# Softmax attention with an FFN behind it: three moves in the tail of a tile's work, and a new order in two steps of nine

## The chip, the cores and the metric

One core of a Trainium2 chip runs the whole kernel. The metric is the device time of one execution in microseconds (us). TensorE (PE, with its weight loads as PEld), VectorE (DVE), ScalarE (ACT), GpSimd (POOL) and SyncE (SP, which issues the DMAs) each work through their own instructions in the order in which the program gives them, and wait for each other by semaphores.

## The reference

Attention for 4 batches and 8 heads, 576 positions, head size 64, with a relative bias from a small network, and a two-layer FFN (512 to 2048 to 512, leaky ReLU) on its output:

```python
scores = scale * np.matmul(q, k.transpose(0, 1, 3, 2)) + bias     # bias: MLP of log-distances, per head
scores = scores - np.max(scores, axis=-1, keepdims=True)
attn = np.exp(scores)
attn = attn / (np.sum(attn, axis=-1, keepdims=True) + 1e-09)
attn_out = np.matmul(attn, v)
# attn_out -> x [2304, 512]
h = x @ w_in
out = np.maximum(0.01 * h, h) @ w_out
```

## The kernel before, in words

A unit is one pair of heads of one batch; there are 16 units (4 head pairs, 4 batches each, the batch running fastest). The 2 x 576 query rows of a unit are cut into nine tiles of 128 rows: A0 B0 A1 B1 M A2 B2 A3 B3 (A and B are the two heads; M holds the last 64 rows of both). `step(n)` is called for n = 0 to 152 and works on three tiles at once. "Step 0" to "step 8" below are n modulo 9.

In a step, TensorE makes the scores of tile n (`qk_mm`, L235; L227 for M). VectorE adds the bias and finds the extremum in one pass (`softmax_a`, L258). ScalarE takes the exponential and its row sums (`softmax_b`, L266). Three steps later `transposes` turns the tile on TensorE (L300, L304, L318) into a PSUM tile `t`, which ScalarE copies to `PT` (L316, L306).

After the first five tiles (M is the last of them) and after the last four (B3 is the last) a half unit is complete. `recip` makes the reciprocals of the row sums on VectorE (L272 adds 1e-9, L273 inverts), and GpSimd spreads them over a tile `rb` (L276, L278) and copies a piece of M (L279). `turn_rb` turns `rb` on TensorE (L305, L289) into the upper half of the PSUM tile `o`, and VectorE copies it to `PT` (L309 twice for M, L290). Then `pv` multiplies with V (L335, 20 matmuls) into the same PSUM tile `o`, columns 0 to 287. L290 reads the whole of that tile. A PV group is issued in step 0 and in step 4, one each. `pv_exit` scales the result on VectorE (L348) a step later.

The first 512 positions of batch 0 (both exits of units 0, 4, 8 and 12) go into FFN block 0's own tiles at once. For them `pv_exit` scales into `xt` (L344), ScalarE rounds it (L345, `hi`), and a step later VectorE subtracts to get the rest (L386, `lo`).

The order is written out by hand. In most steps scores and softmax come first, then transposes and PV. Step 4 (`ahead`) has transposes and PV first. Beside this, step 1 rounds the next unit's q (L194, VectorE) and steps 2 and 3 subtract its rest (L206, GpSimd); step 4 rounds k (L199) and steps 5 and 6 subtract its rest (L209, GpSimd). Three VectorE or ScalarE pieces of the weights' preparation (`fill`) come at the end of step 0 and in step 4. PSUM tiles `s` (scores), `t` and `o` have two buffers each. Before all this the bias tables are made (the first 65 us or so); behind it the FFN runs, its first matmul group (`ffn1(0, 0)`) being issued after step n = 146.

Of the kernel before, what the change touches and what calls it, by code (L numbers as in the profile page):

```python
# [8 lines left out]
F32 = mybir.dt.float32  # L9
# [5 lines left out]
B, H, S, D, HID = 4, 8, 576, 64, 32  # L15
# [10 lines left out]
KINDS = ["A0", "B0", "A1", "B1", "M", "A2", "B2", "A3", "B3"]  # L26
# [3 lines left out]
LAG = 3  # L30
# [6 lines left out]
def attention_ffn(ctx: ExitStack, tc: tile.TileContext, qt, kt, vm, vt, wi, wo, cst, out):  # L37
    nc = tc.nc
# [12 lines left out]
    def pstile(tag):  # L51
        shape = [128, 1024] if tag == "s" else [128, 512]
        return ps.tile(shape, F32, tag=tag, name="ps_" + tag)
# [3 lines left out]
    ident = ap.tile([128, 128], F32, name="ident")  # L57
# [7 lines left out]
    PT = ap.tile([128, 2, 10, HS], F32, name="PT")  # L65
# [23 lines left out]
    def gen_w(T):  # L89
        return max(S - 16 * T, 16 * T + 16)  # L90

    plan, load = [], {"a": 0.0, "v": 5.0}
    for T in GEN:
        w = gen_w(T)
# [79 lines left out]
    def load_unit(u):  # L174
        hp, b = divmod(u, B)
        q_, k_ = raw_b[u % 2]
        for t, src in ((q_, qt), (k_, kt)):
            for p in (0, 64):
                nc.sync.dma_start(out=t[p:p + 64], in_=src[hp, b])
        raw[u] = (q_, k_)  # L180
# [30 lines left out]
    st, pp = {}, {}  # L211

    def tile_id(n):
        u, i = divmod(n, 9)
        return u, KINDS[i]
# [22 lines left out]
    mx_t, sm_t, rb_t, pair = {}, {}, {}, [None]  # L238

    def softmax_a(n):  # L240
        u, kind = tile_id(n)
        hp = u // B
        bt = bias[hp, "M"][:] if kind == "M" else bias[hp, kind[1]][:, 0 if kind[0] == "A" else 1, :]
        col = 1 if kind[0] == "B" else 0
        if col == 0:
            mx_t[n] = ap.tile([128, 2], F32, tag="mx", name="mx", bufs=6)
        else:
            mx_t[n] = mx_t[n - 1]
        g, sc = int(KINDS.index(kind) > 4), 4 if kind == "M" else 2 * (int(kind[1]) % 2) + col
        if kind in ("A0", "A2"):  # L250
            sm_t[u, g] = ap.tile([128, 12], F32, tag="sm", name="sm", bufs=3)
        if kind == "M":
            pair[0] = ap.tile([128, S + 64], F32, tag="pM", name="pM", bufs=1)
        elif col == 0:
            pair[0] = ap.tile([128, 2 * S], F32, tag="p", name="p", bufs=3)
        p = pair[0][:, S * col:S * col + S]
        s_, i = st.pop(n), mx_t[n][:, col:col + 1]
        nc.vector.tensor_tensor_reduce(out=p, in0=s_[:, S0:S0 + S], in1=bt, scale=-0.125, scalar=3.4e38, op0=ALU.add, op1=ALU.min, accum_out=i)  # L258
        pp[n] = pair[0]
        ex_q.append((p, i, sm_t[u, g][:, sc:sc + 1]))  # L260
# [3 lines left out]
    def softmax_b():  # L264
        p, i, sm = ex_q.pop(0)
        nc.scalar.activation(out=p, in_=p, func=AF.Exp, bias=i, scale=-1.0, accum_out=sm)  # L266

    def recip(n):
        u, kind = tile_id(n)
        g = int(kind != "M")  # L270
        sm, w = sm_t.pop((u, g)), 4 if g else 5
        nc.vector.tensor_scalar_add(sm[:, 0:w], sm[:, 0:w], 1e-9)  # L272
        nc.vector.reciprocal(sm[:, 6:6 + w], sm[:, 0:w])  # L273
        rb = rb_t[u, g] = ap.tile([128, 384], F32, tag="rb", name="rb", bufs=2)
        one = sm[:, 6:10].rearrange("p (h o) -> p h o", o=1).to_broadcast([128, 4, 64])
        nc.gpsimd.tensor_copy(rb[:, 0:256].rearrange("p (h c) -> p h c", h=4), one)  # L276
        if g == 0:
            nc.gpsimd.tensor_copy(rb[:, 256:384], sm[:, 10:11].to_broadcast([128, 128]))  # L278
            nc.gpsimd.tensor_copy(pp[n][:, S:S + 64], pp[n][:, S - 64:S])  # L279

    outs = {}
    pv_q = []

    def halves(t):
        return t[:].rearrange("p (a c) -> p a c", a=2)

    def turn_rb(u, g, rb):
        for i in range(2):
            nc.tensor.transpose(outs[u, g][:, 256 + 128 * i:384 + 128 * i], rb[:, 128 * i:128 * i + 128], ident[:])  # L289
        nc.vector.tensor_copy(PT[:, g, 8:10, 0:256], halves(outs[u, g]))  # L290

    def transposes(n, at):
        u, kind = tile_id(n)
        p = pp.pop(n)
        p0 = S + 64 if kind[0] == "B" else 0
        if kind in ("A0", "M"):
            outs[u, int(kind == "M")] = pstile("o")
        t0 = pstile("t")
        for jb in range(4):
            nc.tensor.transpose(t0[:, 128 * jb:128 * jb + 128], p[:, p0 + 128 * jb:p0 + 128 * jb + 128], ident[:])  # L300
        if kind == "M":
            rb = rb_t.pop((u, 0))
            tl = outs[u, 1]
            nc.tensor.transpose(tl[:, 0:128], p[:, 512:640], ident[:])  # L304
            nc.tensor.transpose(tl[:, 256:384], rb[:, 256:384], ident[:])  # L305
            nc.scalar.copy(out=PT[:, :, 0:8, 256:288], in_=t0[:].rearrange("p (j g c) -> p g j c", j=8, g=2))  # L306
            for h in range(2):
                r, c = slice(64 * h, 64 * h + 64), slice(64 * h, 64 * h + 64)
                nc.vector.tensor_copy(PT[r, :, 8:10, 256:288], halves(tl)[r, :, c].rearrange("p a (g c) -> p g a c", g=2))  # L309
            turn_rb(u, 0, rb)  # L310
            pv_q.append((at, u, 0))
            return
        ic, h = int(kind[1]), 0 if kind[0] == "A" else 1
        g, i2 = ic // 2, ic % 2
        c = slice(128 * i2, 128 * i2 + 128)
        nc.scalar.copy(out=PT[:, g, 0:8, c].rearrange("p (j h) c -> p j h c", h=2)[:, :, h, :], in_=t0[:].rearrange("p (j c) -> p j c", j=4))  # L316
        if h == 1:
            nc.tensor.transpose(outs[u, g][:, c], p[:, 512:640], ident[:])  # L318
            if kind == "B3":
                turn_rb(u, 1, rb_t.pop((u, 1)))  # L320
                pv_q.append((at, u, 1))

    x_pend, pv_out = [], []

    def pv():
        _, u, g = pv_q.pop(0)
        hp, b = divmod(u, B)
        o, pt = outs.pop((u, g)), PT[:, g]
        for jb in range(5):
            for h in range(2):  # L330
                if jb < 4:
                    l, r = vv[u][:, jb, 64 * h:64 * h + 64], pt[:, 2 * jb + h, :]
                else:
                    l, r = vt_b[u % 3][:, h, :], pt[:, 8, :]
                nc.tensor.matmul(o[64 * h:64 * h + 64, 0:HS], l, r, start=(jb == 0), stop=(jb == 4))  # L335
        pv_out.append((hp, S * b + HS * g, o, pt[:, 9, :]))

    def pv_exit():
        hp, t0, o, r = pv_out.pop(0)
        c = max(0, min(HS, BLK - t0))  # L340
        if c:
            x = ap.tile([128, HS], F32, tag="xt", name="xt", bufs=2)
            hi, lo = (t[:, t0:t0 + c] for t in xs[0, hp])
            nc.vector.tensor_mul(x[:, 0:c], o[:, 0:c], r[:, 0:c])  # L344
            nc.scalar.copy(out=hi, in_=x[:, 0:c])  # L345
            x_pend.append((lo, x[:, 0:c], hi))
        if c < HS:
            nc.vector.tensor_mul(x1[hp][:, t0 + c - BLK:t0 + HS - BLK], o[:, c:HS], r[:, c:HS])  # L348

    NTILE = 9 * HP * B  # L350

# [8 lines left out]
    def split(n, when):  # L360
        if n // 9 + 1 < HP * B:
            for f, *args in SPL.get(when, ()):
                (split_hi, split_lo)[f](n // 9 + 1, *args)

    def step(n):
        ahead = n % 9 == 4
        for turn in (ahead, not ahead):
            if turn:
                if 0 <= n - LAG < NTILE:
                    transposes(n - LAG, n + 2)  # L370
                if pv_q and pv_q[0][0] <= n:
                    pv()
                continue
            if n < NTILE:
                qk_mm(n)
                if ahead and n // 9 + 2 < HP * B:
                    load_unit(n // 9 + 2)
                if ahead:
                    split(n, "M")
                    fill(n, 3)  # L380
                softmax_a(n)
            if 0 <= n - 1 < NTILE and KINDS[(n - 1) % 9] in ("M", "B3"):
                recip(n - 1)
            while x_pend:
                lo, x, hi = x_pend.pop(0)
                nc.vector.tensor_sub(lo, x, hi.bitcast(F32))  # L386
            while pv_out and not ahead:
                pv_exit()
        while ex_q:
            softmax_b()  # L390
# [113 lines left out]
    with tc.manual_schedule():  # L504
# [6 lines left out]
        for n in range(NTILE + LAG + 6):  # L511
            u, i = divmod(n, 9)
            if u == 0:
                while done < GEN_AT[i]:
                    gen_tick(done)
                    done += 1
                    if done >= 6 and done % 2 == 0 and sp_ops:
                        w = sp_ops.pop(0)
# [25 lines left out]
            if u < HP * B:  # L544
                if u % B == B - 1 and u // B + 1 < HP:
                    c = {1: "0", 2: "1", 3: "M", 4: "2", 6: "3"}.get(i)
# [41 lines left out]
        for j in range(len(seq) + 2):  # L588
            if j < len(seq):
                n, m = seq[j]  # L590
# [58 lines left out]
```

## Time and profile before

| | us |
|---|---|
| median of 3 runs (719.26 to 720.31) | 720.21 |
| the profiled execution's own time | 719.8 |
| its span in the trace | 718.0 |
| PE busy | 698.7 |
| PEld busy | 544.2 |
| DVE busy | 388.8 |
| ACT busy | 362.6 |
| POOL busy | 111.9 |

The span is 1.8 us shorter than the execution. Matmuls are pipelined and their ends are modelled, so "busy" for PE means that work was in flight. The granted clock of TensorE is at full speed in every slice of the span.

### The profile page before, as it was taken

The page shows a single profiled execution, that of the slowest core. Times are in us where ns is not written, and L with a number is a line of the kernel's source. Part 1 is how long each engine was busy: PE and PEld are TensorE (multiplying, and loading weights), DVE is VectorE, ACT ScalarE, POOL GpSimd, SP SyncE. Part 2 cuts the span into 40 slices and gives each one's busy share as a digit, 9 for nine tenths or more (in the row PEclk, how much of TensorE's full clock was granted, in tenths as well). Part 3 has the DMA queues.
Part 4 walks back from the last instruction along what each step waited for, and adds up shares of the span by engine and source line. Part 5 has one row for each costly group of instructions (what it writes and reads, how often), then busy time and mean ns, then how long its engine had stood idle before and what let it go on. Part 6 is the DMA issues. An engine that isn't in the chain of part 4 may idle for free.

```text
span 718.0 us, 11142 instructions
## 1 busy us (share of the span) xinstructions
PE 698.7 (97%) x4192; PEld 544.2 (76%) x4192; DVE 388.8 (54%) x882; ACT 362.6 (50%) x792; POOL 111.9 (16%) x135
## 2 busy tenths in 40 slices
PE   6999999999999999999999999999999999999997
PEld 2346677777767786767888888888888888888996
DVE  7996789898889889749996211122111221112111
ACT  7797778767778777775563221222211231122221
POOL 2103335333444434300000000000000000000000
PEclk9999999999999999999999999999999999999999
DMA  9798557447755864002550010000000010000100
GB/s 231 239 316 243 167 164 226 115 114 214 211 158 127 244 173 125 21 1 65 173 174 29 1 59 0 1 0 30 31 0 1 0 59 1 0 1 1 59 1 30
DMA packets 30262, 68.26 MB, mean 95 GB/s; under 512 B 8192, under 2 KB 8320, under 8 KB 30208
## 3 DMA queue, kind: packets, MB, share of 16 engines
q1 hardware_dynamic: 30208, 67.54, 32.4%
q8 instruction: 33, 0.54, 0.3%
q14 instruction: 21, 0.17, 0.1%
HBM read 51.92 MB, written 15.61 MB: 94 GB/s over the span
## 4 chain that ended last, share of the span: by engine, by line
PE 85%; DVE 9%; ACT 3%; issue 2%; DMA 1%; DVEq 0%; SPq 0%
PE ps_o L466 13%; PE ps_t L466 13%; PE ps_o L335 10%; PE ps_s L494 9%; PE ps_s L493 9%; PE ps_s L492 9%; PE ps_s L235 7%; PE ps_t L300 6%; DVE r L114 2%; PE ps_o L125 2%; PE ps_t L125 1%; DVE p L258 1%; PE ps_s L227 1%; PE ps_s L125 1%; DVE pM L258 1%
## 5 line engine op out<-in xcount | busy, mean ns | idle before, releaser
L481 DVE TENSOR_TENSOR gl<-g,gh 128x512 fp32r<-128x512 f32 (+1 forms) x80 | 51.0, 638 | 266.2 <-ACT g L475 266.2
L494 PE MATMUL ps_s<-woh,gl 128*128 128x512 f32 x288 | 112.1, 389 | 0.3 <-DVE gl L481 0.3
L492 PE MATMUL ps_s<-woh,gh 128*128 128x512 f32 x288 | 112.2, 390 | 0.0
L493 PE MATMUL ps_s<-wol,gh 128*128 128x512 f32 x288 | 112.2, 390 | 0.0
L266 ACT ACTIVATE p<-p,mx 128x576 f32<-128x576 f32 x128 | 100.0, 781 | 7.6 <-DVE mx L258 7.6
L258 DVE CUSTOM_DVE_ANT_0 p<-ps_s,bias 128x576 f32<-128x576 f32 x128 | 94.0, 750 | 15.0 <-PE ps_s L235 12.5
L235 PE MATMUL ps_s<-ks,qs 128*128 128x288 f32 x512 | 99.9, 318 | 1.8 <-DVE mx L258 1.5
L235 PEld LDWEIGHTS ps_s<-ks,qs 128*128 128x128 f32 x512 | 72.1, 189 | 19.5 <-issue 6.0
L474 ACT ACTIVATE gh<-ps_o 128x512 fp32r<-128x512 f32 (+1 forms) x39 | 21.5, 552 | 126.6 <-PE ps_o L466 126.6
L316 ACT COPY PT<-ps_t 128x512 f32<-128x512 f32 x128 | 73.4, 574 | 12.9 <-PE ps_t L300 12.9
L474 ACT ACTIVATE gh<-ps_t 128x512 fp32r<-128x512 f32 (+1 forms) x39 | 21.5, 552 | 112.0 <-PE ps_t L466 111.9
L300 PE MATMUL ps_t<-ident,p 128*128 128x128 f32 x512 | 75.0, 273 | 2.3 <-ACT PT L316 2.3
L335 PE MATMUL ps_o<-PT,v 128*64 128x288 f32 x512 | 69.2, 412 | 0.3
L300 PEld LDWEIGHTS ps_t<-ident,p 128*128 128x128 f32 x512 | 61.1, 140 | 4.5 <-ACT PT L316 3.6
L494 PEld LDWEIGHTS ps_s<-woh,gl 128*128 128x128 f32 x288 | 54.1, 188 | 12.0 <-DVE gl L481 0.7
L492 PEld LDWEIGHTS ps_s<-woh,gh 128*128 128x128 f32 x288 | 54.1, 188 | 10.8
L493 PEld LDWEIGHTS ps_s<-wol,gh 128*128 128x128 f32 x288 | 54.1, 188 | 10.6
L466 PE MATMUL ps_t<-xh,wil 128*128 128x512 f32 (+1 forms) x156 | 57.3, 367 | 0.0
L466 PE MATMUL ps_o<-xh,wil 128*128 128x512 f32 (+1 forms) x156 | 57.3, 367 | 0.0
L466 PE MATMUL ps_t<-xl,wih 128*128 128x512 f32 (+1 forms) x156 | 57.3, 367 | 0.0
L466 PE MATMUL ps_o<-xl,wih 128*128 128x512 f32 (+1 forms) x156 | 57.3, 367 | 0.0
L466 PE MATMUL ps_t<-xh,wih 128*128 128x512 f32 (+1 forms) x156 | 57.2, 367 | 0.0
(109 smaller groups left out, 1098.8 us busy)
## 6 DMA issues: line engine op xcount, KB each, us to landing
raw<-kt SPq DMA_DIRECT2D x32, 304.0 KB, 5.7
raw<-qt SPq DMA_DIRECT2D x32, 288.0 KB, 4.2
raw<-wi SPq DMA_DIRECT2D x16, 512.0 KB, 3.5
raw<-wo SPq DMA_DIRECT2D x16, 512.0 KB, 3.6
scr<-x SPq DMA_DIRECT2D x21, 295.5 KB, 4.2
bias<-scr SPq DMA_DIRECT2D x16, 288.0 KB, 5.4
out<-x SPq DMA_DIRECT2D x18, 256.0 KB, 2.1
v<-vm SPq DMA_DIRECT2D x16, 256.0 KB, 6.3
```

Of the source, the lines that this page charges most:

```text
L235: nc.tensor.matmul(s_[:, S0 + HS * hh:S0 + HS * hh + HS], qs[:, c0:c0 + 128], ks[:, k0 + HS * hh:k0 + HS * hh + HS], start=(j == 0), stop= ...
L258: nc.vector.tensor_tensor_reduce(out=p, in0=s_[:, S0:S0 + S], in1=bt, scale=-0.125, scalar=3.4e38, op0=ALU.add, op1=ALU.min, accum_out=i)
L266: nc.scalar.activation(out=p, in_=p, func=AF.Exp, bias=i, scale=-1.0, accum_out=sm)
L300: nc.tensor.transpose(t0[:, 128 * jb:128 * jb + 128], p[:, p0 + 128 * jb:p0 + 128 * jb + 128], ident[:])
L316: nc.scalar.copy(out=PT[:, g, 0:8, c].rearrange("p (j h) c -> p j h c", h=2)[:, :, h, :], in_=t0[:].rearrange("p (j c) -> p j c", j=4))
L335: nc.tensor.matmul(o[64 * h:64 * h + 64, 0:HS], l, r, start=(jb == 0), stop=(jb == 4))
L466: nc.tensor.matmul(h_[:, :N], w, x[:, :N], start=(j == 0), stop=(j == len(mms) - 1))
L474: nc.scalar.activation(out=gh[:, :N], in_=h_[:, :N], func=AF.Prelu, alpha=0.01)
L481: nc.vector.tensor_sub(gl[:, :N], g[:, :N], gh[:, :N].bitcast(F32))
L492: nc.tensor.matmul(o, gh[:, c], wt[m][2][:], start=(m == 0), stop=False)
L493: nc.tensor.matmul(o, gh[:, c], wt[m][3][:], start=False, stop=False)
L494: nc.tensor.matmul(o, gl[:, c], wt[m][2][:], start=False, stop=(m == MF - 1))
```

## The change

- `recip` is split. The addition of 1e-9 and the copy of M's piece go to a new `sums`, on GpSimd, in the step in which `recip` was; the reciprocals and the spreading of `rb` come one step later (steps 6 and 1 instead of 5 and 0).
- `turn_rb` comes one step later too (steps 8 and 3 instead of 7 and 2), with its VectorE copies (L309, L290). The PV groups stay in steps 0 and 4.
- In steps 1 and 5 (`behind`) transposes, and then `pv_exit`, stand ahead of the scores.
- `x_steps` replaces the old rounding: the ScalarE copy `hi` comes later in its step's order (behind the transposes' copy), the subtraction `lo` a step after it on GpSimd instead of VectorE.

```diff
+    def sums(n):
+        ...
+        nc.gpsimd.tensor_scalar_add(sm[:, 0:w], sm[:, 0:w], 1e-9)
+        if g == 0:
+            nc.gpsimd.tensor_copy(pp[n][:, S:S + 64], pp[n][:, S - 64:S])
     def recip(n):
-        nc.vector.tensor_scalar_add(sm[:, 0:w], sm[:, 0:w], 1e-9)
         nc.vector.reciprocal(sm[:, 6:6 + w], sm[:, 0:w])
         ...
-            nc.gpsimd.tensor_copy(pp[n][:, S:S + 64], pp[n][:, S - 64:S])
-    def turn_rb(u, g, rb):
+    def turn_rb(n, at):
+        ...
+        rb = rb_t.pop((u, g))
+        if g == 0:
+            tl = outs[u, 1]
+            nc.tensor.transpose(tl[:, 256:384], rb[:, 256:384], ident[:])
+            for h in range(2):
+                ...
+                nc.vector.tensor_copy(PT[r, :, 8:10, 256:288], ...)
         for i in range(2):
             nc.tensor.transpose(outs[u, g][:, 256 + 128 * i:384 + 128 * i], ...)
         nc.vector.tensor_copy(PT[:, g, 8:10, 0:256], halves(outs[u, g]))
+        pv_q.append((at, u, g))
@@ pv_exit
-            nc.scalar.copy(out=hi, in_=x[:, 0:c])
+    def x_steps(n):
+        while x_lo:
+            lo, x, hi = x_lo.pop(0)
+            nc.gpsimd.tensor_sub(lo, x, hi.bitcast(F32))
+        while x_pend:
+            lo, x, hi = x_pend.pop(0)
+            nc.scalar.copy(out=hi, in_=x)
+            x_lo.append((lo, x, hi))
@@ step
-        ahead = n % 9 == 4
-        for turn in (ahead, not ahead):
+        ahead, behind = n % 9 == 4, n % 9 in (1, 5)
+        for turn in (ahead or behind, not (ahead or behind)):
             if turn:
                 if 0 <= n - LAG < NTILE:
-                    transposes(n - LAG, n + 2)
+                    transposes(n - LAG)
+                if 0 <= n - LAG - 1 < NTILE and KINDS[(n - LAG - 1) % 9] in ("M", "B3"):
+                    turn_rb(n - LAG - 1, n + 1)
                 if pv_q and pv_q[0][0] <= n:
                     pv()
                 continue
+            while pv_out and behind:
+                pv_exit()
             if n < NTILE:
                 qk_mm(n)
                 ...
                 softmax_a(n)
+            if 0 <= n - 2 < NTILE and KINDS[(n - 2) % 9] in ("M", "B3"):
+                recip(n - 2)
             if 0 <= n - 1 < NTILE and KINDS[(n - 1) % 9] in ("M", "B3"):
-                recip(n - 1)
-            while x_pend:
-                lo, x, hi = x_pend.pop(0)
-                nc.vector.tensor_sub(lo, x, hi.bitcast(F32))
+                sums(n - 1)
+            x_steps(n)
             while pv_out and not ahead:
                 pv_exit()
```

## Rows read from the trace of the kernel before

**Rows 1.** Windows (us; busy by engine; clock, DMA share, GB/s): nine ordinary steps; nine with unit 8's x exits.
```profile
183.03:198.79 15.76, 15.76 (x129) 12.22 (x130) 13.95 (x36) 12.07 (x30) 6.67 (x9) 1.00 0.71 207
198.79:216.59 17.80, 16.50 (x129) 12.23 (x130) 15.40 (x37) 12.62 (x31) 7.20 (x9) 1.00 0.56 156
```
**Rows 2.** Chain that ended last (start, us, what): first and last step-0 PV groups.
```profile
101.98 2.58 PE ps_o L335 x20
...
313.00 2.58 PE ps_o L335 x20
```
**Rows 3.** Timeline (start, us, instruction, idle before), steps 1 to 4.
```profile
185.54 0.56 PEld L235 LDWEIGHTS ps_s<-ks,qs 128*128 128x128 f32 x4 [0.44 <-DVE tmp L434]
...
186.05 0.49 PEld L300 LDWEIGHTS ps_t<-ident,p 128*128 128x128 f32 x4
...
186.38 0.76 DVE L258 CUSTOM_DVE_ANT_0 p<-ps_s,bias 128x576 f32<-128x576 f32 x1 [0.52 <-PE ps_s L235]
186.50 0.57 PEld L235 LDWEIGHTS ps_s<-ks,qs 128*128 128x128 f32 x4
...
187.06 0.45 DVE L348 TENSOR_TENSOR x<-ps_o,PT 128x288 f32<-128x288 f32 x1
...
187.43 0.68 DVE L194 CAST qs<-raw 128x1024 fp32r<-128x1024 f32 x1
...
188.03 0.75 DVE L258 CUSTOM_DVE_ANT_0 p<-ps_s,bias 128x576 f32<-128x576 f32 x1
...
188.70 0.69 DVE L290 COPY PT<-ps_o 128x512 f32<-128x512 f32 x1
...
189.52 1.65 PEld L335 LDWEIGHTS ps_o<-PT,v 128*64 128x64 f32 x16 [0.17 <-DVE PT L290]
```
**Rows 4.** Timeline, steps 4 to 0 of the same unit.
```profile
192.10 0.21 PEld L227 LDWEIGHTS ps_s<-raw,raw 64*64 64x64 f32 x8 [0.44 <-issue]
...
193.81 0.78 ACT L266 ACTIVATE pM<-pM,mx 128x576 f32<-128x576 f32 x1 [1.75 <-DVE mx L258]
...
194.91 0.19 DVE L273 RECIPROCAL sm<-sm 128x5 f32<-128x5 f32 x1
...
195.02 0.42 DVE L348 TENSOR_TENSOR x<-ps_o,PT 128x288 f32<-128x288 f32 x1
...
195.23 0.40 POOL L276 COPY rb<-sm 128x256 f32<-128x256 f32 x1 [4.37 <-DVE sm L273]
...
195.81 0.24 POOL L279 COPY pM<-pM 128x64 f32<-128x64 f32 x1
...
196.00 2.96 POOL L209 TENSOR_TENSOR ks<-raw,ks 128x576 fp32r<-128x576 f32 x2
...
196.10 0.14 PEld L304 LDWEIGHTS ps_o<-ident,pM 128*128 128x128 f32 x1 [0.22 <-POOL pM L279]
...
196.70 0.59 DVE L309 COPY PT<-ps_o 64x128 f32<-64x128 f32 x2
...
198.72 1.65 PEld L335 LDWEIGHTS ps_o<-PT,v 128*64 128x64 f32 x16 [0.17 <-DVE mx L258]
```
**Rows 5.** Timeline, steps 1 to 4 of unit 9, with unit 8's x exit.
```profile
203.31 0.43 ACT L345 CAST xh<-xt 128x288 fp32r<-128x288 f32 x1 [2.43 <-DVE xt L344]
...
204.47 1.23 DVE L386 TENSOR_TENSOR xl<-xt,xh 128x288 fp32r<-128x288 f32 x1
...
205.62 0.68 DVE L290 COPY PT<-ps_o 128x512 f32<-128x512 f32 x1
...
206.35 1.65 PEld L335 LDWEIGHTS ps_o<-PT,v 128*64 128x64 f32 x16 [0.30 <-DVE PT L290]
```
**Rows 6.** Lines of POOL (busy us, mean ns): the one small addition or product.
```profile
L85 POOL TENSOR_SCALAR cs<-cs 128x32 f32<-128x32 f32 x1 | 0.6, 601 | 2.2 <-DMA cs<-cst 2.2
```
**Rows 7.** Timeline, the last PV group behind the FFN's first matmuls.
```profile
316.44 0.25 PEld L289 LDWEIGHTS ps_o<-ident,rb 128*128 128x128 f32 x2
...
319.63 1.65 PEld L335 LDWEIGHTS ps_o<-PT,v 128*64 128x64 f32 x16 [0.35 <-ACT woh L444]
```

More of the change, by code (lines that the diff above doesn't have):

```diff
@@ L266, in softmax_b @@
         nc.scalar.activation(out=p, in_=p, func=AF.Exp, bias=i, scale=-1.0, accum_out=sm)
+    def sums(n):
+        u, kind = tile_id(n)
+        g = int(kind != "M")
+        sm, w = sm_t[u, g], 4 if g else 5
+        nc.gpsimd.tensor_scalar_add(sm[:, 0:w], sm[:, 0:w], 1e-9)
+        if g == 0:
+            nc.gpsimd.tensor_copy(pp[n][:, S:S + 64], pp[n][:, S - 64:S])
     def recip(n):
@@ L285, in halves @@
         return t[:].rearrange("p (a c) -> p a c", a=2)
-    def turn_rb(u, g, rb):
+    def turn_rb(n, at):
+        u, kind = tile_id(n)
+        g = int(kind != "M")
+        rb = rb_t.pop((u, g))
[3 more added lines that the diff above has]
+            for h in range(2):
+                r, c = slice(64 * h, 64 * h + 64), slice(64 * h, 64 * h + 64)
+                nc.vector.tensor_copy(PT[r, :, 8:10, 256:288], halves(tl)[r, :, c].rearrange("p a (g c) -> p g a c", g=2))
         for i in range(2):
@@ L290, in turn_rb, with transposes @@
         nc.vector.tensor_copy(PT[:, g, 8:10, 0:256], halves(outs[u, g]))
-    def transposes(n, at):
+        pv_q.append((at, u, g))
+    def transposes(n):
         u, kind = tile_id(n)
@@ L301, in transposes @@
         if kind == "M":
[L302 to L305, printed above, removed]
+            nc.tensor.transpose(outs[u, 1][:, 0:128], p[:, 512:640], ident[:])
             nc.scalar.copy(out=PT[:, :, 0:8, 256:288], in_=t0[:].rearrange("p (j g c) -> p g j c", j=8, g=2))
[L307 to L311, printed above, removed]
             return
@@ L318, in transposes @@
             nc.tensor.transpose(outs[u, g][:, c], p[:, 512:640], ident[:])
-            if kind == "B3":
-                turn_rb(u, 1, rb_t.pop((u, 1)))
-                pv_q.append((at, u, 1))
     x_pend, pv_out = [], []
@@ L348, in pv_exit @@
             nc.vector.tensor_mul(x1[hp][:, t0 + c - BLK:t0 + HS - BLK], o[:, c:HS], r[:, c:HS])
+    x_lo = []
+    def x_steps(n):
[6 more added lines that the diff above has]
+            x_lo.append((lo, x, hi))
     NTILE = 9 * HP * B
```

## The prediction

> **What bounds the kernel now.** I read the windows first, with their borders at the PV groups of step 0. Nine ordinary steps take 15.76 us, and PE has work in flight for all of it, while DVE is busy for 13.95 [rows 1]. The nine steps that hold the x exits of unit 8 take 17.80 us for the same 129 matmul records, and there PE is in flight for 16.50 only [rows 1]. The chain that ended last shows how many there are of each: from the step-0 group at 101.98 to that at 313.00 it is 211.0 us for 13 intervals [rows 2]; with three x intervals (units 4, 8, 12) at 17.80, the other ten come to 157.6, or 15.76 each. So attention runs at PE's pace, with DVE little behind, and four units (unit 0 too) lose some 2.0 us each to the x work. A stall of PE is not made up anywhere: it adds to the time.
>
> The timeline shows where a stall is near. I count from P, where PE's weight loads are free of the step-0 group (185.54). The next PV group, in step 4, starts at P + 3.98 (189.52). DVE's L290 ends 0.13 us before it, at P + 3.85 (188.70 + 0.69) [rows 3]. That the group waits for L290 is seen beside unit 8's exits: L290 ends at 206.30, the group starts at 206.35, with an idle time of 0.30 put down to L290 [rows 5]. The code has the reason: L290 reads the whole PSUM tile `o` into whose columns 0 to 287 the group's first matmul writes. So **L290 has 0.13 us to spare, and 0.05 is used by the semaphore**.
>
> **First half: from the step-0 group to the step-4 group.** The diff moves L290 behind the softmax pass of step 3 on DVE, puts the reciprocal ahead of the rounding of q in step 1, and lets the scores of step 1 wait for a set of transposes. The old chain on DVE is: softmax 1 starts at P + 0.84, then L348, L194, softmax 2, L290. The new one, with slots read as start to start [rows 3]:
>
> - four transposes first: 186.05 to 186.50, 0.45; the scores are then 0.84 from done: softmax 1 starts at P + 1.29;
> - softmax 1: 186.38 to 187.06, 0.68, to 1.97;
> - the reciprocal, 194.91 to 195.02, 0.11 [rows 4], to 2.08;
> - L194: 187.43 to 188.03, 0.60, to 2.68;
> - softmax 2: 188.03 to 188.70, 0.67, to 3.35;
> - softmax 3, as softmax 1, 0.68, to 4.03 (its scores are ready earlier: PE has done two sets of scores and two of transposes by 2.05, the third set's end is at 2.05 + 0.84 = 2.89);
> - L290, 0.69, to 4.72, and the semaphore, 0.05: the group starts at P + 4.77.
>
> L348 drops out of this chain, since it now runs while PE transposes. PE itself gets to the group no later than at P + 3.98: nothing was added to its work. So PE **stalls for 4.77 - 3.98 = 0.79 us** in each ordinary unit. What the bounds are: if the reciprocal counts with its full 0.19 [rows 4] it is 0.87; if L290 could go in the gap ahead of softmax 3 (it can't by the order) it would be 0.1. I take 0.79.
>
> **Second half: from the step-4 group to the step-0 group.** I count from Q, where PE is free of the step-4 group (192.10); the step-0 group starts at Q + 6.62 (198.72) [rows 4]. Two things go well. The 0.22 us for which L304 waits on GpSimd's copy L279 goes [rows 4], since that copy now stands ahead of `rb`; and DVE no longer waits for ScalarE ahead of L272, which frees DVE, not PE.
>
> What comes late is `rb`. GpSimd's order was L276, L278, L279 and then twice L209 [rows 4]. Now it is the addition and L279 (step 5), the first L209 (end of step 5), L276 and L278 (step 6), the second L209. The exponential of M ends at 193.81 + 0.78 and 0.1 for its sum: Q + 2.58 [rows 4]. The addition of 128x5 on GpSimd is nowhere in the trace. The nearest rows are the copy of 128x64, 0.24 [rows 4], and a product of 128x32, 0.60 [rows 6]; I take 0.24, as with five columns it is nearer to the smaller, and keep 0.1 to 0.6. With 0.05 for the semaphore it ends at 2.87, L279 at 3.11, the first L209 (half of 2.96) at 4.59, L276 and L278 (195.23 to 195.81, and 0.06 to the end) at 5.23. PE would be at the turned reciprocals by about Q + 4.85: 196.10 is Q + 4.00, less the wait of 0.22, with one M transpose (0.11, a quarter of a set), one set of scores (0.51) and one of transposes (0.45) behind it [rows 3, 4]. It stalls there until 5.28. Then 0.11 for a transpose and 0.33 until DVE reads (186.05 to 186.38 [rows 3]), L309 twice, 0.59, L290, 0.69, and 0.05: the group starts at 7.05, late by 0.43. If the addition takes 0.6, it is 0.79; if `rb` is there in time, DVE's own order (softmax 8 until about 5.37, then 0.59, 0.69, 0.05) still gives 6.70, late by 0.08. I take 0.45, with 0.08 to 0.79.
>
> No DMA is issued by a moved step, and SP's queue is as before. Behind the waiting addition stand both L209; the second ends near Q + 6.8, and its k is first used in step 1 of the next unit, after P. In the first half the same moves cost nothing on GpSimd: `rb` of B3 is asked for at P + 3.0, and GpSimd has nothing else from the reciprocal (2.1) on.
>
> An ordinary unit thus costs **0.79 + 0.45 = 1.24 us more**, 17.0 instead of 15.76.
>
> **The x exits.** Before, ScalarE's copy `hi` waits 2.43 us for DVE's L344 at the head of ScalarE's queue, the next transposes' copy stands behind it, and the subtraction L386 holds DVE for 1.23 us ahead of L290 [rows 5]. After, L344 is early, `hi` stands behind the transposes' copy, and the subtraction is on GpSimd. From L209's 128x576 (1.48) 288 columns are 0.74, an estimate; GpSimd is busy for 6.67 of 15.76 [rows 1], so it fits. Then these four intervals become ordinary ones at 17.0: 17.80 - 17.00 = 0.80 less each, **3.2 us less**. The bound on the other side is that 0.7 us of GpSimd work ahead of `rb` makes an x interval 0.7 longer: 2.8 in all.
>
> A rule of the Trainium skill bears on this (SBUF — State Buffer, "SBUF: two separate sides"): one pair of SBUF ports is shared by VectorE and GpSimd, and whichever of an instruction of GpSimd and one of VectorE with two SBUF inputs (or in a two-port mode) starts first holds it, while the other stands still. The trace agrees as far as it goes: L386 has two SBUF inputs and takes 1.23 us beside L206, L348 of the same size reads PSUM and takes 0.45 [rows 3, 5]. What it would do to the reciprocal is the second rival.
>
> **The ends.** The last unit has no next q and k to round: in its first half the chain ends 0.4 to 0.6 earlier, in its second `rb` is in time. Some 0.7 in all, by the same sums. The last group of all stood behind the FFN's first matmuls, with its turned `rb` ahead of them at 316.44 [rows 7]; now its transposes come behind them, 0.22 before 319.63, and 0.3 for their end, 0.69 for L290, 0.05: it starts near 320.6 instead of 319.63, 0.95 later. The FFN behind it is as before and moves as a whole. The work ahead of the first step-0 group is bound by the bias tables; I put it at nothing, within 0.5 both ways.
>
> **The sum.** Ten ordinary intervals (nine of those ten from 101.98 on, and the one ahead of them): 10 x 1.24 = 12.4. Four x intervals: -3.2. Last unit 0.7, last group 0.95. In all +10.9 us on the profiled execution's own 719.8 (span 718.0 and 1.8 around it): 730.7; the median of the runs is 0.4 above that execution. I predict **731.0 us**.
>
> **Rivals.**
>
> 1. *The reciprocal is held by the port too.* The reciprocal of step 6 comes while the first L209 runs (Q + 3.11 to 4.59). If it must wait for its end, then softmax 7 starts at 4.70, softmax 8 ends at 6.06, L309 and L290 at 7.34, and the group starts at 7.39 instead of 7.05. That is 0.34 more for 14 units: 735.8. For it: L386's 1.23 us. Against: no row shows a one-input operation of five columns beside GpSimd.
> 2. *`rb` in time.* GpSimd is quicker, or PE later, than I have it: only 0.08 is lost in the second half. 10 x 0.87 - 4 x 1.17 + 0.6 + 0.95 = +5.6: 725.4. For it: the margin is only 0.4 us.
> 3. *Faster.* The mechanism: L290 keeps up. DVE had 0.52 us idle ahead of softmax 1 [rows 3] and gets rid of L272's waits and of L386; if that let it finish L290 before P + 3.93 and Q + 6.57, the gains would stand alone: 4 x 2.04 for x and 0.22 for each of 15 waits of L304, -11.5: 708.3. It decides at L290's end, 0.79 us from where I have it. Against: the freed idle time lies ahead of the scores of step 1, and the chain starts with those scores.
> 4. *The x intervals gain nothing*, because the subtraction on GpSimd delays `rb` or `lo`: 731 + 2.8 = 734.
> 5. *The stalls and gains cancel*: both halves lose a half of what I say, 0.6 a unit: +6.2 - 5.7 + 1 = about 721.
>
> **How the numbers follow.** Forecast 0.58, rival 1 0.13, rival 2 0.12, rival 3 0.09, rival 4 0.04, rival 5 0.04. A difference of 0.2% (1.4 us) is about what a measurement here can tell from none. Slower: forecast, 1, 2 and 4, 0.87; same: rival 5, 0.04; faster: 0.09. The range takes in the bounds of the addition (0.36 x 14 = 5 us up), rival 1 and rival 2 with 2 us below: 723 to 738; outside are the faster case and half of what cancels, and some of the sums' own error.
>
> **What would show it.** Right: ordinary intervals near 17.0; PE idle ahead of the first L335 of both groups, put down to L290; L290 behind softmax 3 and softmax 8 on DVE; L305 waiting for GpSimd's L278; no wait of L304 for L279; x intervals as long as ordinary ones; L386's successor on GpSimd at about 0.7 us. Wrong: intervals of 15.8, or the step-4 group starting within 4.1 us of P. If the reciprocal of step 6 takes over 1 us, it is rival 1.

## The result, and the profile after

The change makes the kernel slower: 729.91 us median of 4 runs (728.33 to 733.17) against 719.8 of before on the same chip, a ratio of 1.0146 with a 95% interval of 1.0106 to 1.0186. Forecast were 731.0 and a range of 723 to 738. The profiled execution of the changed kernel took 733.17 us, with a span of 731.4; it is the slowest of the four, for a reason in the bias tables' stretch that is told below.

Line numbers have moved: old L273 (reciprocal) is L280, L276 and L278 (spreading) are L283 and L285, L305 and L289 (turning) are L299 and L304, L309 and L290 (VectorE copies to `PT`) are L302 and L305, L335 (PV) is L340, L348 (the PV exit) is L352; the transposes L300 are L316, L318 (the transpose into `o`) is L326, and ScalarE's copy L316 is L324; L272 is now GpSimd's addition, L274 its copy of M's piece.

The windows of the changed kernel, with borders at the step-0 groups, answer to [rows 1]: an ordinary unit, and the one with unit 8's x exits (us; busy by engine; clock, DMA share, GB/s).

```profile
191.63:208.44 16.81, 15.95 (x126) 12.13 (x127) 13.87 (x34) 12.17 (x29) 7.62 (x10) 1.00 0.66 192
208.44:225.25 16.81, 16.20 (x127) 12.17 (x127) 14.60 (x35) 12.50 (x31) 9.18 (x12) 1.00 0.57 154
```

Both take 16.81 us. The ordinary unit has grown by 1.05 and PE now has 0.86 us with nothing in flight; the x unit has shrunk by 0.99 and is an ordinary one. DVE's busy time is hardly changed in the ordinary unit (13.95 to 13.87): the engine does nearly the same work, at another time.

The timeline of the changed kernel, steps 1 to 4, answers to [rows 3] (start, us, instruction, idle before and its releaser).

```profile
194.20 0.42 PEld L316 LDWEIGHTS ps_t<-ident,p 128*128 128x128 f32 x4 [0.44 <-issue]
...
194.35 0.46 DVE L352 TENSOR_TENSOR x<-ps_o,PT 128x288 f32<-128x288 f32 x1 [0.57 <-PE ps_o L340]
...
195.43 0.76 DVE L258 CUSTOM_DVE_ANT_0 p<-ps_s,bias 128x576 f32<-128x576 f32 x1 [0.62 <-PE ps_s L235]
...
196.11 0.17 DVE L280 RECIPROCAL sm<-sm 128x4 f32<-128x4 f32 x1
196.20 0.66 DVE L194 CAST qs<-raw 128x1024 fp32r<-128x1024 f32 x1
...
196.78 0.75 DVE L258 CUSTOM_DVE_ANT_0 p<-ps_s,bias 128x576 f32<-128x576 f32 x1
...
197.45 0.75 DVE L258 CUSTOM_DVE_ANT_0 p<-ps_s,bias 128x576 f32<-128x576 f32 x1
...
198.13 0.69 DVE L305 COPY PT<-ps_o 128x512 f32<-128x512 f32 x1
...
198.87 1.65 PEld L340 LDWEIGHTS ps_o<-PT,v 128*64 128x64 f32 x16 [0.72 <-DVE PT L305]
```

P is 194.20 here. From 195.43 on DVE has no gap: softmax 1, the reciprocal, the rounding of q, softmax 2, softmax 3, L305, which ends at 198.82. The step-4 group starts 0.05 later, at P + 4.67, after an idle 0.72 of the weight loads put down to L305. Before it was P + 3.98. The freed DVE time is in the row of L352: an idle 0.57 and another 0.62 around it, ahead of the scores of step 1, where it can't help.

The timeline of the changed kernel, steps 4 to 0, answers to [rows 4].

```profile
201.45 0.21 PEld L227 LDWEIGHTS ps_s<-raw,raw 64*64 64x64 f32 x8 [0.44 <-issue]
...
204.15 0.24 POOL L272 TENSOR_SCALAR sm<-sm 128x5 f32<-128x5 f32 x1 [4.43 <-ACT pM L266]
...
204.45 0.24 POOL L274 COPY pM<-pM 128x64 f32<-128x64 f32 x1
204.64 1.44 POOL L209 TENSOR_TENSOR ks<-raw,ks 128x576 fp32r<-128x576 f32 x1
...
204.67 0.18 DVE L280 RECIPROCAL sm<-sm 128x5 f32<-128x5 f32 x1
...
206.02 0.40 POOL L283 COPY rb<-sm 128x256 f32<-128x256 f32 x1
...
206.36 0.29 POOL L285 COPY rb<-sm 128x128 f32<-128x128 f32 x1
...
206.70 0.14 PEld L299 LDWEIGHTS ps_o<-ident,rb 128*128 128x128 f32 x1 [0.49 <-POOL rb L285]
...
207.07 0.59 DVE L302 COPY PT<-ps_o 64x128 f32<-64x128 f32 x2 [0.25 <-PE ps_o L299]
...
207.69 0.69 DVE L305 COPY PT<-ps_o 128x512 f32<-128x512 f32 x1
...
208.44 1.65 PEld L340 LDWEIGHTS ps_o<-PT,v 128*64 128x64 f32 x16 [0.35 <-DVE PT L305]
```

Q is 201.45. GpSimd runs without a gap from the addition to L285, with the first L209 in the middle; PE's L299 waits for L285 until Q + 5.25; L302 and L305 follow on DVE; the step-0 group starts at Q + 6.99 instead of 6.62. The small addition takes 0.24 us, as assumed from the copy of 128x64. The reciprocal at 204.67 runs in 0.18 us while L209 is running: nothing holds it.

The last two groups, in the chain of waits of the changed kernel, answer to the end of [rows 2] and to [rows 7]: 7.65 us apart, where before it was 319.70 - 313.00 = 6.70 in the same view.

```profile
325.33 2.65 PE ps_o L340 x20
...
332.98 2.66 PE ps_o L340 x20
```

**The first group.** What makes this execution longer than the others is ahead of 75 us. The timeline of the changed kernel and three windows show it.

```profile
69.40 0.76 DVE L258 CUSTOM_DVE_ANT_0 p<-ps_s,bias 128x576 f32<-128x576 f32 x1 [2.10 <-DMA bias<-scr]
70.09 0.58 DVE L302 COPY PT<-ps_o 64x128 f32<-64x128 f32 x2
...
70.73 0.47 PE L326 MATMUL ps_o<-ident,p 128*128 128x128 f32 x1 [2.15 <-DVE PT L302]
...
71.45 4.08 PE L340 MATMUL ps_o<-PT,v 128*64 128x288 f32 x16 [0.25 <-DVE PT L305]
```

```profile
68.00:68.50 0.50, 0.50 (x6) 0.34 (x3) 0.00 (x0) 0.50 (x3) 0.00 (x0) 1.00 1.03 259
68.50:69.00 0.50, 0.08 (x1) 0.00 (x0) 0.00 (x0) 0.23 (x1) 0.00 (x0) 0.53 0.95 202
70.00:75.00 5.00, 4.03 (x17) 2.04 (x19) 2.02 (x7) 2.21 (x5) 0.23 (x1) 0.50 0.58 135
```

In the first unit the softmax of step 8 waits for a bias transfer. L302 now stands behind that softmax on DVE, a transpose on PE (L326, into the tile that L302 reads) behind L302, and PE idles for 2.15 us (68.58 to 70.73) after an earlier 1.46 (65.89 to 67.35). The granted clock is 1.00 until 68.5 us and then 0.50, the lower of its two levels (1.2 GHz), until 75: it fell as the second idle time began, and so not because of it. The profiled executions of E4 and E5 (below) fell to the lower level in the same stretch after idle times of 1.38 and 1.60 us, with none behind step 8's softmax in E4 and 0.67 in E5. At that clock the first PV group takes 4.56 us in the chain of waits, as against 2.65 or 2.66 for all later ones. With the group starting at 71.45 instead of 67.91, this execution loses 3.5 + 1.9 = 5.4 us there. Without it the span would be 726.0, and the two fastest executions have spans of 726.5 and 726.9.

### The profile page after: what moved, and what is told of

Read it like the earlier page. It is cut to its first block, busy times and chain, and to the rows that moved or that the text cites. A ratio compares the mean times of both kernels' runs of the same rounds, so it can differ in the third digit from the quotient of the medians.

```text
span 731.4 us, 11158 instructions
## 1 busy us (share of the span) xinstructions
PE 702.6 (96%) x4192; PEld 544.4 (74%) x4192; DVE 380.7 (52%) x842; ACT 363.4 (50%) x792; POOL 131.7 (18%) x175
## 4 chain that ended last, share of the span: by engine, by line
PE 76%; DVE 11%; DMA 5%; issue 4%; SPq 2%; ACT 1%; POOL 1%; DVEq 0%; POOLq 0%; ACTq 0%
PE ps_o L485 13%; PE ps_t L485 13%; PE ps_o L340 10%; PE ps_s L513 9%; PE ps_s L511 9%; PE ps_s L512 9%; PE ps_s L235 3%; PE ps_t L316 3%; DVE PT L305 3%; DVE r L114 2%; DMA bias<-scr 2%; DVE p L258 2%; PE ps_o L125 2%; PE ps_t L125 2%; PE ps_s L227 1%
## 5 line engine op out<-in xcount | busy, mean ns | idle before, releaser
L235 PE MATMUL ps_s<-ks,qs 128*128 128x288 f32 x512 | 92.7, 313 | 2.0 <-DVE mx L258 2.0
L324 ACT COPY PT<-ps_t 128x512 f32<-128x512 f32 x128 | 73.2, 573 | 20.0 <-PE ps_t L316 20.0
L340 PE MATMUL ps_o<-PT,v 128*64 128x288 f32 x512 | 71.1, 421 | 9.8 <-DVE PT L305 8.1
L316 PE MATMUL ps_t<-ident,p 128*128 128x128 f32 x512 | 79.3, 278 | 0.5 <-ACT PT L324 0.2
L316 PEld LDWEIGHTS ps_t<-ident,p 128*128 128x128 f32 x512 | 58.5, 140 | 18.3 <-issue 10.9
L340 PEld LDWEIGHTS ps_o<-PT,v 128*64 128x64 f32 x512 | 34.8, 139 | 37.1 <-DVE PT L305 16.4
```

The lines of the kernel that those rows point to most:

```text
L235: nc.tensor.matmul(s_[:, S0 + HS * hh:S0 + HS * hh + HS], qs[:, c0:c0 + 128], ks[:, k0 + HS * hh:k0 + HS * hh + HS], start=(j == 0), stop= ...
```

## The experiments

Times are medians; "before" is 719.8 to 720.0 in each comparison. E1 and E3 do one part of the change alone, E2 does two.

**E1: the x part alone**

```diff
 # before.py, plus:
-            nc.scalar.copy(out=hi, in_=x[:, 0:c])
+    def x_steps(n): ...                 # as in the change
-            while x_pend: ... nc.vector.tensor_sub(lo, x, hi.bitcast(F32))
+            x_steps(n)
```

> The kernel before with only the x part of the change (hi a step later on ScalarE, lo a step after it on GpSimd). Theory (L290 on DVE gates the PV groups, the x part is a gain): the four x intervals fall from 17.80 to about 15.8, ordinary ones stay at 15.76; time 719.8 - 4 x 2.0 = 712. Rival (a subtraction on GpSimd delays rb or the next unit's rests as much as it saves): x intervals stay above 17, time 717 to 720.

Measured: 713.94 us, ratio 0.9919 (0.9902 to 0.9935). The windows: an ordinary unit, then unit 4's and unit 8's x units.

```profile
116.70:132.46 15.76, 15.76 (x128) 12.21 (x127) 13.54 (x35) 12.59 (x30) 6.95 (x9) 1.00 0.71 204
132.46:148.87 16.41, 16.10 (x128) 12.19 (x127) 14.92 (x37) 12.28 (x31) 8.19 (x10) 1.00 0.52 133
196.37:212.35 15.98, 15.98 (x127) 12.21 (x126) 14.77 (x37) 12.31 (x31) 7.95 (x10) 1.00 0.57 161
```

Ordinary units are untouched, x units lose 1.4 to 1.8 of their 2.0 us of excess; all of it was expected. The x part is a gain of some 6 us.

**E2: the later step, with `sums` on GpSimd**

```diff
 # after.py with the old x rounding, and:
-        ahead, behind = n % 9 == 4, n % 9 in (1, 5)
+        ahead, behind = n % 9 == 4, False
```

> The change without its x part and without the new order in steps 1 and 5: only sums on GpSimd, reciprocals and turn_rb a step later. Theory: both stalls are here. The step-4 group starts near P + 4.6 (before 3.98, after 4.67), ordinary intervals 16.7 to 16.9, x intervals above 18; time 734 to 737. Rival (the order in steps 1 and 5, which sets the scores behind transposes, is what makes softmax and L290 late): ordinary intervals 15.8 to 16.2, time 720 to 725.

Measured: 736.69 us, ratio 1.0244 (1.0222 to 1.0266). Its windows, with borders at the step-0 groups:

```profile
190.73:207.64 16.91, 15.84 (x126) 12.23 (x126) 13.78 (x34) 12.06 (x29) 7.31 (x10) 1.00 0.66 189
207.64:226.21 18.57, 16.72 (x126) 12.18 (x126) 15.51 (x37) 12.78 (x31) 7.66 (x10) 1.00 0.54 147
```

Time and intervals are as expected. Ordinary units cost 1.15 more than before, x units 0.77 more. All of the loss is here; `sums` has no part in it, as E7 shows.

**E3: the new order in steps 1 and 5 alone**

```diff
 # before.py, plus:
-        ahead = n % 9 == 4
-        for turn in (ahead, not ahead):
+        ahead, behind = n % 9 == 4, n % 9 in (1, 5)
+        for turn in (ahead or behind, not (ahead or behind)):
 ...
+            while pv_out and behind:
+                pv_exit()
```

> The kernel before with only the new order in steps 1 and 5 (transposes and the PV exit ahead of the scores); the x rounding is the old one and its subtraction now falls into the same step. Theory: softmax 1 starts 0.45 later but L348 leaves the chain, so L290 ends near P + 3.9 and ordinary intervals stay at 15.8 to 15.9; x intervals 18 to 18.5; time 720 to 723. Rival (this order is the cost): ordinary intervals 16.3 or more, time above 727.

Measured: 716.01 us, ratio 0.9955 (0.9939 to 0.9972), faster than I expected.

```profile
181.19:197.10 15.91, 15.91 (x127) 12.11 (x127) 14.04 (x36) 12.18 (x29) 6.67 (x9) 1.00 0.67 197
197.10:213.43 16.33, 16.03 (x127) 12.13 (x126) 14.51 (x37) 12.73 (x31) 6.83 (x9) 1.00 0.62 164
```

Ordinary units cost 0.15 more; up to 0.14 was expected. The x units I had wrong: they fall from 17.80 to 16.33 though the subtraction is still on VectorE and still ahead of L290. The timeline of unit 8's exit shows how (the subtraction is L388 here).

```profile
200.37 0.59 ACT L316 COPY PT<-ps_t 128x512 f32<-128x512 f32 x1 [1.14 <-PE ps_t L300]
...
200.85 0.44 ACT L345 CAST xh<-xt 128x288 fp32r<-128x288 f32 x1
...
201.58 0.45 DVE L388 TENSOR_TENSOR xl<-xt,xh 128x288 fp32r<-128x288 f32 x1
...
202.87 2.50 POOL L206 TENSOR_TENSOR qs<-raw,qs 64x512 fp32r<-64x512 f32 x2 [3.89 <-PE ps_s L235]
```

`hi` stands behind the transposes' copy on ScalarE and holds up nobody, and the subtraction comes while GpSimd is idle: it takes 0.45 us, where beside L206 it took 1.23 [rows 5]. So most of the x gain can be had by this order as well; how much of it is `hi`'s place and how much the shorter subtraction, no run separates. E11 asks the same from another side.

**E4: B3's turned reciprocals ahead of the scores of step 3**

```diff
 # after.py
+        if 0 <= n - LAG - 1 < NTILE and KINDS[(n - LAG - 1) % 9] == "B3":
+            turn_rb(n - LAG - 1, n + 1)
         for turn in (ahead or behind, not (ahead or behind)):
             ...
-                if 0 <= n - LAG - 1 < NTILE and KINDS[(n - LAG - 1) % 9] in ("M", "B3"):
+                if 0 <= n - LAG - 1 < NTILE and KINDS[(n - LAG - 1) % 9] == "M":
                     turn_rb(n - LAG - 1, n + 1)
```

> The changed kernel, with the turned reciprocals of B3 (transposes and L305, the old L290) ahead of the scores of step 3, so that on DVE the copy stands ahead of softmax 3 again. Theory: the step-4 group starts near P + 4.05 instead of 4.67; ordinary intervals 16.81 - 0.6 = 16.2; time 728.3 - 15 x 0.6 = 719.5. Rival (the group waits for something else, such as the transposes' copies on ScalarE): the group stays within 0.15 of P + 4.67, time 727 to 730.

Measured: 733.82 us (1.0190, 1.0167 to 1.0213). Neither the theory nor the rival came about; the timeline of steps 1 to 4 (P is 192.62) shows why.

```profile
194.62 0.66 DVE L194 CAST qs<-raw 128x1024 fp32r<-128x1024 f32 x1
...
194.83 0.70 POOL L283 COPY rb<-sm 128x256 f32<-128x256 f32 x1 [3.75 <-PE ps_t L316]
...
195.58 0.44 PE L304 MATMUL ps_o<-ident,rb 128*128 128x128 f32 x2 [0.69 <-POOL rb L283]
...
196.06 0.69 DVE L305 COPY PT<-ps_o 128x512 f32<-128x512 f32 x1
...
197.46 2.16 PE L340 MATMUL ps_o<-PT,v 128*64 128x288 f32 x16
```

DVE's L305 is out of the group's way, it ends at 196.75, 0.71 ahead of the group. But PE now asks for `rb` at once and waits 0.69 us for GpSimd's L283, which ends at 195.53. It takes 0.70 instead of 0.40 and ends 0.25 us after L194, beside which it runs (in E6, where L194 has gone from there, L283 takes 0.40). With the reciprocal a step later, neither of the two places tried for the turn in step 3 is both early enough for DVE and late enough for GpSimd. The stall moved; the group starts at P + 4.84, and an ordinary unit takes 16.98 us (190.04 to 207.02).

**E5 and E6: one member taken out of each chain; E8: both**

```diff
 # E5, after.py: k's rest a step later, behind rb on GpSimd
-SPL = {... 5: [(1, "k", 0)], 6: [(1, "k", 1)]}
+SPL = {... 6: [(1, "k", 0)], 7: [(1, "k", 1)]}
 # E6, after.py: q rounded at the end of step 0
-SPL = {1: [(0, "q")], ...
+SPL = {0: [(0, "q")], ...
 # E8: both
```

> The changed kernel, with GpSimd's two subtractions for the next unit's k (L209) a step later (steps 6 and 7), so that L283 and L285, which spread the reciprocals, come ahead of them. Theory: PE no longer waits for rb in step 8 (0.48 of idle weight loads ahead of L299 goes), the step-0 group starts near Q + 6.65 instead of 6.99; ordinary intervals 16.81 - 0.3 = 16.5; time 728.3 - 14 x 0.3 = 724. Rival (DVE's softmax 8 and the copies are late by themselves, rb is not what ends last): the group stays at Q + 6.9 to 7.0, time 728 to 730.

> The changed kernel, with the rounding of the next unit's q (L194, 0.66 on DVE) at the end of step 0 instead of step 1. It is one member of the chain from softmax 1 to L305. Theory (the step-4 group waits at the end of that DVE chain): softmax 3 is then bound by its scores (ready about P + 2.9), L305 ends near P + 4.27 and the group starts at P + 4.3 instead of 4.67; ordinary intervals about 16.45; time 728.3 - 15 x 0.35 = 723. Rival (the group waits for the turned reciprocals or for ScalarE's copies): it stays at P + 4.6 to 4.7, time 728 to 730.

> The changed kernel with both: q rounded at the end of step 0, k's rest in steps 6 and 7. Theory: the two stalls are in different halves and add: ordinary intervals about 16.15; time near 719. Rival (one stall only hides the other): no more than the better of the two alone.

Measured: E5 726.95 us (1.0101, 1.0085 to 1.0118), E6 724.57 (1.0064, 1.0047 to 1.0081), E8 722.45 (1.0041, 1.0028 to 1.0054). An ordinary unit of E5, of E6 and of E8, one window each:

```profile
187.75:204.23 16.48, 15.97 (x128) 12.20 (x127) 13.79 (x34) 12.17 (x30) 7.48 (x11) 1.00 0.68 195
```

```profile
186.28:202.71 16.43, 15.96 (x126) 12.16 (x126) 14.00 (x34) 12.09 (x29) 7.30 (x10) 1.00 0.68 196
```

```profile
168.53:184.62 16.09, 15.96 (x127) 12.20 (x126) 13.60 (x33) 12.64 (x31) 7.14 (x11) 1.00 0.78 218
```

16.5, 16.45 and 16.15 were expected. In E5 the step-0 group starts at Q + 6.67 (197.56 to 204.23, expected 6.65), and L299's wait for L285 is gone; in E6 the step-4 group starts at P + 4.29 (188.86 to 193.15, expected 4.3), right behind L305:

```profile
192.41 0.69 DVE L305 COPY PT<-ps_o 128x512 f32<-128x512 f32 x1
...
193.15 0.93 PEld L340 LDWEIGHTS ps_o<-PT,v 128*64 128x64 f32 x10 [0.36 <-DVE PT L305]
```

The savings of 0.33 and 0.38 add to 0.72 in E8. E5's and E8's medians are 3 and 3.5 us above what I expected. In E5's profiled execution the first group again ran at a lowered clock. The x units of both did not shrink with the ordinary ones: those of units 4, 8 and 12 take 17.1 to 17.3 us in E5 and 16.75 to 16.95 in E8, where the changed kernel has 16.8 to 16.9. There GpSimd's subtraction for `lo` stands ahead of k's rest, and the next unit's first scores wait for that rest (L209) for 0.69 us in E5 (unit 8, 220.33), where in ordinary units they wait for 0.25. The two halves are separate chains, and both end where the prediction put them.

**E7: x part and sums, without the later step**

```diff
 # before.py with the x part of E1, and in recip:
-        nc.vector.tensor_scalar_add(sm[:, 0:w], sm[:, 0:w], 1e-9)
+        nc.gpsimd.tensor_scalar_add(sm[:, 0:w], sm[:, 0:w], 1e-9)
+        if g == 0:
+            nc.gpsimd.tensor_copy(pp[n][:, S:S + 64], pp[n][:, S - 64:S])
         nc.vector.reciprocal(sm[:, 6:6 + w], sm[:, 0:w])
         ...
-            nc.gpsimd.tensor_copy(pp[n][:, S:S + 64], pp[n][:, S - 64:S])
```

> The kernel before with two parts of the change only: the x part, and the addition and M's piece on GpSimd ahead of rb, with the reciprocals and turn_rb in the steps in which they were. Theory: beside the x gain, PE's wait of 0.22 ahead of L304 goes, since M's piece no longer stands behind rb: 713.9 (the x part alone) - 15 x 0.2 = 711. Rival (DVE now waits for GpSimd's addition ahead of the reciprocals, and L309 and L290 come late): 714 to 717.

Measured: 712.47 us, ratio 0.9898 (0.9884 to 0.9913): faster than both kernels, by 7.5 and 17 us.

```profile
179.99:195.59 15.60, 15.60 (x128) 12.24 (x127) 13.62 (x34) 12.23 (x29) 7.17 (x11) 1.00 0.71 207
195.59:211.45 15.86, 15.86 (x127) 12.23 (x127) 14.40 (x35) 12.55 (x31) 8.52 (x12) 1.00 0.61 165
```

An ordinary unit falls to 15.60, 0.16 below that of before: of the 0.22 of L304, 0.16 is gained. Between E1 and E7 the medians differ by 1.5 us, in different comparisons; the windows carry the claim, not the medians.

**E9: the first unit alone**

```diff
 # after.py
-        ahead, behind = n % 9 == 4, n % 9 in (1, 5)
+        ahead, behind = n % 9 == 4, n % 9 in (1, 5) or n == 8
```

> The changed kernel, with transposes and turned reciprocals ahead of the scores in the eighth step of the first unit alone (n = 8), so that L302 on DVE no longer stands behind a softmax that waits for a bias transfer. Theory (in the slower executions of the changed kernel the first PV group is late and then runs at half the granted clock, because PE stands idle for over 2 us behind that softmax): the clock stays at 1.00 between 66 and 74 us, time 726.5 to 728.5, and executions lie within 1 us. Rival (the late bias transfer costs the same wherever it is waited for): 728 to 733 as the changed kernel.

Measured: 727.91 us (726.98 to 728.14), against 729.91 (728.33 to 733.17) of the changed kernel. Its windows over the stretch in question:

```profile
66.00:70.00 4.00, 3.06 (x25) 2.08 (x25) 3.29 (x9) 2.31 (x6) 0.61 (x2) 1.00 1.02 251
70.00:74.00 4.00, 4.00 (x34) 3.35 (x31) 2.23 (x6) 3.04 (x8) 1.06 (x3) 1.00 0.69 158
```

The clock stays at 1.00 and the executions lie within 1.2 us. The reason given for the lower clock does not hold, though: in the changed kernel the clock had fallen when the idle time behind step 8's softmax began, and in E4 it fell without one. What this order does shorten is the idle time before: 0.94 us instead of 1.46. In this profile no softmax waited for a second bias transfer, so that a late one would cost nothing in this order is not seen in a trace. Four executions are few for it: longer executions with a lower mean clock come without the later step too, 722.46 us (0.997) as one of eleven of the kernel before and 715.88 (0.997) as one of six of E10.

**E10: all but the later step**

```diff
 # after.py
-            if ... KINDS[(n - 2) % 9] in ("M", "B3"):
-                recip(n - 2)
             if ... KINDS[(n - 1) % 9] in ("M", "B3"):
                 sums(n - 1)
+                recip(n - 1)
 ...
-                if ... KINDS[(n - LAG - 1) % 9] in ("M", "B3"):
-                    turn_rb(n - LAG - 1, n + 1)
+                if ... KINDS[(n - LAG) % 9] in ("M", "B3"):
+                    turn_rb(n - LAG, n + 2)
```

> The changed kernel with reciprocals and turn_rb back in the steps in which they were (sums on GpSimd, the x part, and the new order in steps 1 and 5 stay). Theory: the later step is all of the loss. Ordinary intervals 15.6 to 15.9, x intervals 15.7 to 16.1, time 711 to 713. Rival (part of the loss is in what stays): above 716.

Measured: 713.30 us, ratio 0.9909 (0.9892 to 0.9927), 0.3 above the expected range.

```profile
179.91:195.61 15.70, 15.70 (x127) 12.13 (x126) 13.63 (x34) 12.19 (x29) 7.18 (x11) 1.00 0.71 205
195.61:211.75 16.14, 15.87 (x127) 12.14 (x126) 14.47 (x37) 12.68 (x31) 8.09 (x13) 1.00 0.58 163
```

Undoing the later step in the changed kernel turns 1.5% slower into 0.9% faster. From the two sides, E2 and E10, the later step is worth 17 us.

**E11: the x part with `lo` on VectorE**

```diff
 # E1, but in x_steps:
-            nc.gpsimd.tensor_sub(lo, x, hi.bitcast(F32))
+            nc.vector.tensor_sub(lo, x, hi.bitcast(F32))
```

> The kernel before with hi and lo later as in the change, but with lo's subtraction still on VectorE. Theory (the x gain comes from ScalarE's and VectorE's order, hi no longer at the head of ScalarE's queue and lo no longer ahead of L290): x intervals 16.0 to 16.5, time 713 to 716. Rival (the gain comes from taking 1.2 to 1.6 us off VectorE, where the subtraction stands still beside GpSimd): x intervals 17.0 or more, time 717 to 719.

Measured: 714.29 us, ratio 0.9919 (0.9905 to 0.9933), the same as E1 (713.94). The x unit of unit 8 takes 16.20 us, and its subtraction on VectorE is about as slow as it was, 1.20 us beside L206. (It comes in two shapes; the four of 128x288 take 1.20 us on average, where it was 1.23, the four of 128x224 take 0.92, where it was 1.58.)

```profile
195.91:212.11 16.20, 16.04 (x127) 12.21 (x126) 14.62 (x37) 12.54 (x31) 6.89 (x9) 1.00 0.60 164
```

```profile
202.92 1.20 DVE L354 TENSOR_TENSOR xl<-xt,xh 128x288 fp32r<-128x288 f32 x1
```

So the x gain comes from when the two instructions stand in their queues, and not from the engine: behind softmax 3 and L290 (in step 3) unit 8's x unit is 0.44 us longer than an ordinary one with the subtraction on VectorE (E11) and 0.22 with it on GpSimd (E1), where it was 2.04.

## Why the prediction was right

- *What bounds, and L290's margin.* Right. The step-4 group starts 0.05 behind the end of L305, and E6 moves it by moving one member of the chain ahead of it. That the tile `o` is the reason for the wait was read from the code; no run gave the copy another tile, so that is argued, not shown.
- *First half.* P + 4.77 was forecast, 4.67 measured: a stall of 0.69 instead of 0.79. The term that was too large is the start of softmax 1, at P + 1.23 instead of 1.29: with the transposes ahead, the loads of the scores follow after 0.39 (194.20 to 194.59), and not the 0.45 that I took from the old order; two slots on DVE (the reciprocal and L194) were 0.02 shorter each.
- *Second half.* Q + 7.05 forecast, 6.99 measured, each link within 0.1: the addition's end at 2.94, L285's at 5.20, L299 at 5.25 (5.28). I then took 0.45 where my own sum gave 0.43, and 0.37 was right. E5 bears out what would be left with `rb` in time (0.08 forecast, 6.67 - 6.62 = 0.05 measured).
- *The x exits.* Forecast -0.80 each, measured -0.99, as the ordinary units grew less. But the reason was incomplete: the engine to which `lo` went does not matter (E11), its place does, and the new order in steps 1 and 5 alone gives 1.47 of the 2.04 (E3), though it leaves `lo` ahead of L290, where it takes 0.45. GpSimd's subtraction of 288 columns takes 0.80 us as a mean of four, where 0.74 was estimated from L209.
- *The ends.* The last group 0.95 later, as forecast. For the first unit I had nothing, within 0.5; it costs from nothing to 5.4 us, by execution. That mechanism was not in the prediction.
- *The sum.* Ten ordinary units at 1.05, four x units at -0.99, 0.7 and 0.95 for the ends: +8.2, so 728.0 on the execution of 719.8. (That takes one unit of each kind for all. From the first PV group's start to the last's it was 251.7 us, 67.90 to 319.63, and is 261.5, 71.44 to 332.94; less the 1.9 of the low clock that is +7.9.) The fastest two executions are at 728.3 and 728.7. So the steady part was over-forecast by 2.7 us, and the first unit, not forecast, brought the median up towards my number: 731.0 against 729.9 is in part luck, nearer than the terms deserve.
- *The rivals.* The held reciprocal (rival 1; the sentence on the port calls it the second) is refuted by its row (0.18 us beside L209). `rb` in time, faster, the x units gaining nothing, and stalls and gains that cancel did not come about.

The port rule of the Trainium skill (SBUF — State Buffer, "SBUF: two separate sides") fits the rows with two operands or a wide copy: the subtraction takes 0.45 with GpSimd idle (E3) and 1.23 beside L206, L283 takes 0.70 instead of 0.40 beside L194 (E4). The small reciprocal, with one SBUF input, was not held.

## What to carry to other kernels

Before a step is moved back to take a wait out of one engine's queue, find the last reader that its result has, and count what then stands ahead of it on every queue on the way: here the copy behind the reciprocals had 0.08 us to spare, and one softmax pass ahead of it was enough. Idle time that is freed ahead of the input of a chain does not shorten the chain. Instructions that nobody waits for soon (here `hi` and `lo`) could be moved back with a gain, on whichever engine; those that gate the busiest engine could not.

## What the runs showed of the hardware

- In the changed kernel's profiled execution the granted clock was 1.00 until 68.5 us and at its lower level (0.50) from there to 75; the PV group in that stretch took 4.56 instead of 2.65 us. Before it fell PE had idled for 1.46 us and worked for 1.23; the 2.15 us of idling came behind the fall. In E4 and E5 it fell behind idle times of 1.38 and 1.60 us; in the kernel before and in E8, with 1.18 and 1.21 in the same stretch, it stayed at 1.00.
- An addition of 128x5 on GpSimd takes 0.24 us with VectorE on PSUM, as much as a copy of 128x64. That of 128x4 takes 0.23 us at 71.16 of the changed kernel, with VectorE on PSUM too, and 0.44 at 192.22, beside VectorE's L451, which reads and writes SBUF.
